# Shift product in the bank of the column sums, and the sums' logarithm and exponential ahead of the next unit's first exponential

## The chip, the cores and the metric

One core of a Trainium2 chip runs the kernel. The time is the device time of one execution in microseconds (us); three runs of the kernel before gave 409.75, 409.88 and 410.16 us, a median of 409.88 us. Engines: PE is TensorE, DVE is VectorE, ACT is ScalarE, POOL is GpSimd, SP is SyncE (here it only issues DMAs).

## What is computed

The reference is an attention with normalised queries and keys, followed by a two-layer network over its output:

```python
q_n, k_n = rmsnorm(q, g_q), rmsnorm(k, g_k)            # 8 batches, 12 heads, 448 rows, 64 wide
scores = matmul(q_n, k_n.T) / 8
attn = exp(scores - max(scores)); attn = attn / (sum(attn) + 1e-9)
x = matmul(attn, v) -> (3584, 768)
h = x @ w_in                                            # (768, 2048)
out = maximum(0.01 * h, h) @ w_out                      # (2048, 768), float32
```

## The kernel before

**Units.** The attention is cut into 24 units (`NU`): 8 batches of three groups of four heads. Unit u has seven key tiles. Scores are made transposed (keys on the partitions, queries along the row), so the sum that divides a query's row is a sum over partitions, and TensorE makes it with matmuls against ones. Every score tile covers two PSUM banks and goes through one exponential on ACT (`ex`, line 243, 128x896 elements), which writes the tile `et` to SBUF.

**The shift.** The exponentials of a unit need one number `eb`, a bound on its scores, the same on all partitions. It is made at the start of the unit from the first score tile: DVE takes the maximum of each partition (line 257), multiplies an identity matrix by it (`dg`, line 259), TensorE multiplies ones by `dg` so that all 128 maxima lie along the row on every partition (`shift_mm`, line 264), DVE takes the maximum along that row (line 274) and turns it into `eb` (line 284). The product needs 128 free columns in PSUM. For units 4 to 23 it goes into 64 spare columns (448 to 511) of each of the two banks that hold the PV product of the unit before: two matmuls of 64 columns (line 271).

**The unit before.** In the first step of unit u the kernel also ends unit u-1. `pv_slot` makes the product of `et` with the values into two banks (28 matmuls, line 400). `zcol` makes the column sums in one bank of their own, in columns 0 to 223 (line 337; up to 28 matmuls, fewer where DVE has added some tiles first in `add_e`, line 322). `pv_out` copies the PV product to SBUF (`x32`; on DVE at line 350 for the units 3 to 6, on ACT at line 352 for the others). `zcol_ln` takes the logarithm of the sums on ACT (line 358), `zcol_inv` the exponential of its negative (line 363), which is the reciprocal, and SP then issues four DMAs that spread it over the partitions into `rz` (line 368). At last x32 times rz is written to `xt` (line 378): on POOL for nine units (`xmul_pool`), on DVE for eleven (`xmul_sb`). `xt` is the input of the network.

**The network.** Its matmuls (first layer line 422, second layer line 521 and 468, late batches line 655) lie as items in a list (`queue`). After each of the four steps d = 0..3 of unit u, `fill(u, d, jobs)` runs as many items as a table (`PLAN`) says, and after each item one of `jobs`: DVE and ACT work for later units, loads and the like. Most items first call `flush()`, which issues the DVE and ACT work that earlier items put off: the additions that take products out of PSUM (line 528), and the sums `sa` of parts of the first layer's output (lines 502 to 511), which the second layer's matmuls read. In late batches an addition or a copy out of a bank (line 674) has to be done before the next product is accumulated into that bank.

**Order of the work.** The program is issued in the order in which it is written (`manual_schedule`); each engine runs its own instructions in that order, and waits on semaphores for other engines. Banks are handed out from a list of free ones: `aux()` takes one bank, `slot()` takes a pair, `drop()` gives them back at the end of the list. Instructions of different engines on the same bank wait for each other even where they touch different columns.

In the first step of unit u = 4..23 (line 1048 on) the order is: scores of tile 0, the shift's maximum and `dg`, `flush`, then the lines

```python
pv_slot(u - 1)
zcol(u - 1)
shift_mm(u)
pv_out(u - 1)
```

then `ex(u, 2)`, then `zcol_ln(u - 1)`, and then `fill` with the jobs; `zcol_inv(u - 1)` is the first job (after the first item), and `load(u + 4)`, the DMAs that fetch the queries and keys of a later unit, is the next. In the last unit (u = 23) `zcol_inv` is a job of the second step. POOL's work in this step is a small copy that waits for a transposed tile (line 290) and the DMA that loads later values (`load_v`, line 155).

Of the kernel before, what the change touches and what calls it, by code (L numbers as in the profile page):

```python
# [8 lines left out]
FP32 = mybir.dt.float32  # L9
FP16 = mybir.dt.float16  # L10
AF = mybir.ActivationFunctionType
ALU = mybir.AluOpType
AXL = mybir.AxisListType
# [5 lines left out]
def kernel(  # L19
# [11 lines left out]
    nc = tc.nc  # L31

    B, H, S, D = q.shape
    QH = 4
    NS = 7
    P = 128
    NQ = H // QH
    NU = B * NQ
# [9 lines left out]
    small = ctx.enter_context(tc.tile_pool(name="small", bufs=2))  # L48
# [39 lines left out]
    def drop(tile_):  # L88
        for i in range(8):
            if tile_ is single[i]:  # L90
                assert i not in free
                free.append(i)
                return
        x = [i for i in range(4) if tile_ is double[i]][0]
        assert 2 * x not in free and 2 * x + 1 not in free
        free.extend((2 * x, 2 * x + 1))
# [9 lines left out]
    onesp = cst.tile([P, P], FP16)  # L106
# [32 lines left out]
    st = {}  # L139
# [91 lines left out]
    def qk(u, steps):  # L231
        st[u]["sT"] = []
        for t in steps:
            sT = slot()
            score(u, t, (sT[:, 0], sT[:, 1]))
            st[u]["sT"].append((t, sT))
# [24 lines left out]
    def shift_bank(u):  # L261
        st[u]["pb"] = aux()

    def shift_mm(u):
        s = st[u]
        peak = s["spare"][:, 510:511]
        own = s.get("own")
        if own is not None or u > 0 and "pslot" in st[u - 1]:
            pb = (st[u - 1]["pslot"] if own is None else own)[:, :, S:S + 64]
            for x in range(2):  # L270
                nc.tensor.matmul(pb[:, x], onesp, s["dg"][:, 64 * x:64 * x + 64], start=True, stop=True)  # L271
            if own is not None:
                peak = small.tile([P, 1], FP32, tag="peak", name="peak")
            nc.vector.tensor_reduce(peak, pb, axis=AXL.XY, op=ALU.max)  # L274
        else:
            if "pb" not in s:
                shift_bank(u)
            pb = s["pb"]
            nc.tensor.matmul(pb[:, 0:P], onesp, s["dg"], start=True, stop=True)
            nc.vector.tensor_reduce(peak, pb[:, 0:P], axis=AXL.X, op=ALU.max)  # L280
            if u >= 3:
                drop(pb)
        s["eb"] = small.tile([P, 1], FP32, tag="eb", name="eb")
        nc.vector.tensor_scalar(s["eb"], peak, -1.0, DELTA, op0=ALU.mult, op1=ALU.add)
# [61 lines left out]
    def pv_out(u):  # L346
        s = st[u]
        s["x32"] = zpool.tile([P, 2, S], FP32, tag="x32", name="x32")
        if u in (3, 4, 5, 6):
            nc.vector.tensor_copy(s["x32"], s["pslot"][:, :, 0:S])  # L350
        else:
            nc.scalar.copy(s["x32"], s["pslot"][:, :, 0:S])  # L352
        drop(s["pslot"])

    def zcol_ln(u):
        s = st[u]
        s["zs"] = zpool.tile([P, HS], FP32, tag="zs", name="zs")
        nc.scalar.activation(s["zs"], s["zc"][:, 0:HS], AF.Ln)
        drop(s["zc"])

    def zcol_inv(u):
        s = st[u]
        nc.scalar.activation(s["zs"], s["zs"], AF.Exp, bias=0.0, scale=-1.0)
        s["rz"] = zpool.tile([P, 2, S], FP32, tag="rz", name="rz")
        for r in range(2):
            for y in range(2):
                src = s["zs"][64 * y + r:64 * y + 64:2, None, :]
                nc.sync.dma_start(s["rz"][:, r, HS * y:HS * y + HS], src.broadcast_to([32, 4, HS]))  # L368
# [421 lines left out]
    def narrow(u):  # L790
        return 3 <= u < NU - 1
# [43 lines left out]
    with tc.manual_schedule():  # L835
# [208 lines left out]
        for u in range(3, NU):  # L1044
            for d in range(4):
                if u == 5 and d == 0:
                    shared.append(u)
                if d > 0 or u > 3:
                    qk(u, (TRIPLES if tripled(u) else STEPS)[d])
                    if d == 0:  # L1050
                        shift_max(u)
                        flush()
                        if u in (5, 6):
                            xmul_sb(u - 2)
                        if narrow(u - 1):
                            pv_slot(u - 1)
                            zcol(u - 1)
                            shift_mm(u)
                            pv_out(u - 1)
                        else:  # L1060
                            zsum_slot(u - 1)
                            pv(u - 1)
                            shift_mm(u)
                            zinv(u - 1)
                    ex(u, 2)
                    if d == 0 and narrow(u - 1):
                        zcol_ln(u - 1)
                if d == 2 and (u == 3 or ADDED.get(u, 0) > 3) and u < NU - 1:
                    add_e(u)
                    if u > 4:  # L1070
                        xmul_sb(u - 1)
                jobs = []

                def job(fn, *args):
                    jobs.append(lambda: fn(*args))

                if d == 0:
                    if u == 3:
                        prep_norm(4)
                        gate(4)  # L1080
                    elif narrow(u - 1):
                        if u < NU - 1:
                            job(zcol_inv, u - 1)
                    else:
                        xmul(u - 1)
                    if u + 4 < NU:
                        job(load, u + 4)
                    if u < 5:
                        load_v(u + 3)
                    if u < 6:  # L1090
                        prep_sqp(u + 3)
                    if 5 <= u < NU - 3:
                        gate_t_of(u + 1)
                        load_v(u + 3)
                if d == 1 and narrow(u - 1) and not 5 <= u < 8 and ADDED.get(u, 0) < 4:
                    xmul_pool(u - 1)
                if u == NU - 1:
                    if d == 1:
                        job(zcol_inv, u - 1)
                if fed(u, d) and u > 3:  # L1100
                    push(u // NQ - 1)
                if (u, d) in ((3, 1), (4, 0)):
                    for ti in range(2):
                        prep_tr(u + 1, ti, VV)
                if u + 2 < NU:
                    if d == 1:
                        if ADDED.get(u) == 3 and u > 3:
                            job(lambda u: (prep_ssq(u + 2), add_e(u)), u)
                        else:
                            for ti in range(2):  # L1110
                                job(prep_ssq, u + 2, ALL, (ti,))
                if d == 1 and 5 <= u < NU - 1:
                    job(prep_g, u + 1)
                if u + 2 < NU:
                    if d == 2:
                        job(prep_rinv, u + 2)
                        if u == 6:
                            job(xmul_sb, u - 1)
                        for ti in range(2):
                            job(prep_norm, u + 2, ALL, (ti,))  # L1120
                        if u > 3:
                            job(prep_trd, u + 2)
                if d == 1 and 4 <= u < 8:
                    job(weight_sum, u - 4, 0)
                if d == 0 and 5 <= u < 9:
                    job(weight_sum, u - 5, 1)
                if d == 1 and u == NU - 2:
                    jobs.append(lambda: None)
                    job(add_e, u)
                if u == NU - 2 and d == 0:  # L1130
                    for n, tile_ in ((1, (raws, "rq", 3)), (2, (raws, "rk", 3)), (3, None), (4, (prep_p, "sq", 3))):
                        job(win_sum, n, 1, tile_)
                    for n in (3, 1, 2, 4):
                        job(x_sum, LATE, n)
                if u == NU - 1 and d == 3:
                    job(add_e, u)
                    job(xmul_sb, u - 1)
                if d == 3 and 6 <= u < NU - 3:
                    for ti in range(2):
                        job(prep_sq, u + 3, ALL, (ti,))  # L1140
                if st[u]["sT"]:
                    n = 1 if d == 1 and u % 6 == 2 else 0
                    jobs[n:n + 1] = [also(lambda: ex(u), *jobs[n:n + 1])]
                fill(u, d, jobs)
# [39 lines left out]
```

## Time and profile before

| | |
|---|---|
| median of three runs | 409.88 us |
| the profiled execution's own time | 409.67 us |
| its span, first to last instruction | 407.9 us |
| PE busy | 396.9 us (97%), clock granted 1.0 throughout |
| DVE busy | 307.1 us (75%) |
| ACT busy | 300.6 us (74%) |
| POOL busy | 72.9 us (18%) |

The profiled execution took 1.8 us more than its span. A page of the profile gives busy times of each engine, the chain of work that ended last (followed back from the last instruction), the costliest groups of instructions (a group's line, engine, operation, output and inputs; busy time and mean duration; then the idle time of the engine just before them, with what ended it), and the DMAs. The timeline lists start, duration, engine, line and operation; a bracket at the end of a line is the engine's idle time before it and what ended that. PE's records overlap: a matmul's record is longer than its distance to the next.

### The profile page before, as it was taken

What the parts mean: (1) busy time and instruction counts of PE and PEld (TensorE: products, weight loads), DVE (VectorE), ACT (ScalarE), POOL (GpSimd) and SP (SyncE); (2) the same over time, 40 slices, a digit from 0 to 9 for tenths busy, and PEclk for the clock granted to TensorE, in tenths of its full rate; (3) what the DMA queues carried; (4) which work ended last, traced back from release to release, by engine and by line L of the source; (5) the groups of instructions that cost most, each with busy time, mean ns of one, the idle gap of its engine ahead of it and who ended that gap; (6) DMA issues with size and microseconds to landing.
All of it is one profiled execution on the core that took longest, in us unless ns stands there. A gap on an engine that the chain in (4) does not pass through costs nothing.

```text
span 407.9 us, 9571 instructions
## 1 busy us (share of the span) xinstructions
PE 396.9 (97%) x3896; PEld 224.9 (55%) x3896; DVE 307.1 (75%) x481; ACT 300.6 (74%) x474; POOL 72.9 (18%) x86
## 2 busy tenths in 40 slices
PE   8999999999999999999999999999999999999996
PEld 7665454544455544555455544554455557559963
DVE  5887999959879665867679766777579888567672
ACT  5998877787978599778878689867996667743600
POOL 1887431200020200020021200021011202000000
PEclk9999999999999999999999999999999999999999
DMA  6999999898664984677664894776752560022023
GB/s 199 277 240 249 240 234 248 212 189 185 164 159 85 251 227 73 178 198 163 164 145 78 230 223 103 195 181 142 170 100 47 124 151 18 16 71 79 2 55 99
DMA packets 72526, 62.87 MB, mean 154 GB/s; under 512 B 36388, under 2 KB 67620, under 8 KB 72484
## 3 DMA queue, kind: packets, MB, share of 16 engines
q1 hardware_dynamic: 61888, 50.08, 46.8%
q0 software_dynamic: 10272, 11.80, 18.4%
q8 instruction: 30, 0.49, 0.5%
q10 hardware_dynamic: 324, 0.39, 0.3%
q14 instruction: 12, 0.10, 0.1%
HBM read 45.61 MB, written 11.01 MB: 139 GB/s over the span
## 4 chain that ended last, share of the span: by engine, by line
PE 80%; ACT 3%; DVE 3%; issue 2%; DMA 1%; SPq 1%; ACTq 0%; DVEq 0%
PE banks L422 27%; PE banks L521 23%; PE banks L228 8%; PE banks L655 6%; PE banks L400 6%; PE banks L468 6%; PE banks L337 3%; ACT et L243 1%; DMA rq<-in_q_dram 1%; SPq L368 1%; PE banks L271 1%; ACT gt L416 1%; DVE banks L257 1%; ACT sq L175 0%; PE banks L210 0%
## 5 line engine op out<-in xcount | busy, mean ns | idle before, releaser
L243 ACT ACTIVATE et<-banks,eb 128x896 f16<-128x896 f32 x168 | 161.4, 1015 | 28.9 <-PE banks L228 18.3
L422 PE MATMUL banks<-xt,win 128*128 128x448 f16 x612 | 122.4, 353 | 1.0 <-DVE xt L378 1.0
L422 PEld LDWEIGHTS <-win 128*128 128x128 f16 x612 | 57.3, 98 | 57.2 <-issue 8.0
L416 ACT ACTIVATE gt<-banks 128x448 f16<-128x448 f32 x104 | 56.4, 563 | 5.1 <-PE banks L422 3.9
L186 DVE TENSOR_REDUCE ssq<-sq 128x14 f32<-128x896 f32 (+2 forms) x49 | 50.3, 1057 | 0.7 <-ACT sq L175 0.7
L228 PE MATMUL banks<-qkT 64*64 64x448 f16 x672 | 49.3, 361 | 1.5 <-DVE qkT L810 0.8
L521 PEld LDWEIGHTS <-sa 128*128 128x128 f16 x352 | 33.4, 98 | 24.6 <-issue 3.6
L521 PE MATMUL banks<-tw,sa 128*128 128x384 f16 x264 | 46.9, 326 | 0.1
L528 DVE TENSOR_TENSOR ost<-banks,ost 128x384 f32<-128x384 f32 x55 | 30.4, 552 | 16.3 <-PE banks L521 14.3
L257 DVE TENSOR_REDUCE banks<-banks 128x1 f32<-128x896 f32 x24 | 26.3, 1097 | 14.2 <-PE banks L228 10.6
L400 PE MATMUL banks<-et,vt 64*64 64x448 f16 x672 | 36.9, 349 | 0.0
L521 PEld LDWEIGHTS <-gt 128*128 128x128 f16 x264 | 25.5, 98 | 18.7 <-issue 2.2
L468 PE MATMUL banks<-wout,gt 128*128 128x384 f16 x192 | 33.7, 327 | 0.0
L198 DVE TENSOR_TENSOR n<-rq,rinv 128x896 f16<-128x896 f32 (+2 forms) x25 | 31.0, 1241 | 3.1 <-ACT rinv L192 3.1
L228 PEld LDWEIGHTS <-qkT 64*64 64x64 f16 x672 | 16.9, 105 | 29.5 <-issue 22.5
L521 PE MATMUL banks<-wout,gt 128*128 128x384 f16 x176 | 32.4, 327 | 0.0
L290 POOL COPY gate_t<-qkT 128x1 f16<-128x1 f16 x16 | 4.8, 299 | 153.5 <-DMA qkT<-n 153.5
L378 POOL TENSOR_TENSOR xt<-x,rz 128x896 f16<-128x896 f32 x9 | 19.0, 2109 | 72.7 <-DMA rz<-zs 67.0
L352 ACT COPY x<-banks 128x896 f32<-128x896 f32 x16 | 14.5, 906 | 21.5 <-DVE banks L274 21.5
L198 DVE TENSOR_TENSOR n<-rk,rinv 128x896 f16<-128x896 f32 (+2 forms) x26 | 26.1, 1011 | 0.0
L400 PEld LDWEIGHTS <-vt 64*64 64x64 f16 x672 | 20.0, 107 | 10.0
L468 PEld LDWEIGHTS <-gt 128*128 128x128 f16 x192 | 17.8, 98 | 13.7 <-issue 2.9
(106 smaller groups left out, 484.7 us busy)
## 6 DMA issues: line engine op xcount, KB each, us to landing
rq<-in_q_dram SPq DMA_DIRECT2D x24, 448.0 KB, 4.8
rk<-in_k_dram SPq DMA_DIRECT2D x24, 448.0 KB, 5.3
out_dram<-ost SPq DMA_DIRECT2D x52, 192.0 KB, 3.4
rz<-zs SPq DMA_DIRECT2D x80, 112.0 KB, 2.8
vt<-in_v_dram POOLq DMA_DIRECT2D x24, 224.0 KB, 4.5
win<-in_moe_w_in_dram POOLq DMA_DIRECT2D x8, 384.0 KB, 14.9
wout<-in_moe_w_out_dram POOLq DMA_DIRECT2D x2, 1536.0 KB, 28.6
out_dram<-ost SPq DMA_DIRECT2D x4, 96.0 KB, 2.1
```

What stands on the lines that cost most here:

```text
L186: nc.vector.tensor_reduce(buf(u, "ssq")[:, ti, :, c[0]:c[1]], buf(u, f"sq{ti}")[:, :, c[0]:c[1]], axis=AXL.X, op=ALU.add)
L198: nc.vector.tensor_tensor(buf(u, "n16")[:, ti, c[0]:c[1]].rearrange("p s a d -> p a s d"), src[:, :, c[0]:c[1]], buf(u, "rinv")[:, ti, :, ...
L228: nc.tensor.matmul(banks[a][64 * r:64 * r + 64, 0:S].rearrange("p (t x) -> p t x", t=NS), kT(u, r, a, t), qT(u, r, a), start=True, stop=True)
L243: nc.scalar.activation(s["et"][:, t], sT[:, :, 0:S], AF.Exp, bias=s["eb"], scale=1.0)
L257: nc.vector.tensor_reduce(s["spare"][:, 511:512], sT[:, :, 0:S], axis=AXL.XY, op=ALU.max)
L400: nc.tensor.matmul(s["pv"][r][64 * a:64 * a + 64, 0:S], vts[u % NV][64 * r:64 * r + 64, a, t], s["et"][64 * r:64 * r + 64, t, a], start=(t ...
L416: nc.scalar.activation(dst, src, AF.Prelu, bias=0.0, scale=1.0, alpha=0.01)
L422: nc.tensor.matmul(hps[:, 0:S], win16[:, kt // 2, kt % 2, ts(ft, P)], xt[:, kt // 2, kt % 2], start=(kt == 0), stop=(kt == KT - 1))
L468: nc.tensor.matmul(op2[:, 0:HC], gt[:, ft, ds(col(t), P)], wout16[:, ft, ds(HC * half, HC)], start=(i == 0), stop=(i == FT - 1))
L521: nc.tensor.matmul(bank[:, 0:HC], a[:, f], b[:, f], start=(first and f == 0), stop=(f == HF - 1), skip_group_check=not first)
L528: nc.vector.tensor_tensor(dst, g[name][:, 0:HC], src, op=ALU.add)
L655: nc.tensor.matmul(bank[:, HX * i:HX * i + HX].rearrange("p (t x) -> p t x", t=NS), w, x[:, kt], start=start, stop=(kt == HK - 1), skip_gr ...
```

## The change

The shift's product of units 4 to 23 goes into the bank of the column sums of the unit before, columns 256 to 383, as one matmul of 128 columns, and DVE's maximum reads it there. The logarithm and the exponential of the column sums, with the four DMAs, are issued right after `pv_out`, ahead of `ex(u, 2)`, for all units but the last; `zcol_inv` is no longer a job of the first step, so the other jobs of that step each follow one item earlier. For u = 23 the logarithm stays behind `ex` and the exponential in the second step. The bank of the column sums is given back before that of the first score tile, so the list of free banks has another order from there on.

```diff
-        if own is not None or u > 0 and "pslot" in st[u - 1]:
-            pb = (st[u - 1]["pslot"] if own is None else own)[:, :, S:S + 64]
+        if own is not None:
+            pb = own[:, :, S:S + 64]
             for x in range(2):
                 nc.tensor.matmul(pb[:, x], onesp, s["dg"][:, 64 * x:64 * x + 64], start=True, stop=True)
-            if own is not None:
-                peak = small.tile([P, 1], FP32, tag="peak", name="peak")
+            peak = small.tile([P, 1], FP32, tag="peak", name="peak")
             nc.vector.tensor_reduce(peak, pb, axis=AXL.XY, op=ALU.max)
+        elif u > 0 and "zc" in st[u - 1]:
+            pb = st[u - 1]["zc"][:, 2 * P:3 * P]
+            nc.tensor.matmul(pb, onesp, s["dg"], start=True, stop=True)
+            nc.vector.tensor_reduce(peak, pb, axis=AXL.X, op=ALU.max)
         else:
...
                             zcol(u - 1)
                             shift_mm(u)
                             pv_out(u - 1)
+                            if u < NU - 1:
+                                zcol_ln(u - 1)
+                                zcol_inv(u - 1)
                         else:
...
                     ex(u, 2)
-                    if d == 0 and narrow(u - 1):
+                    if d == 0 and u == NU - 1:
                         zcol_ln(u - 1)
...
-                    elif narrow(u - 1):
-                        if u < NU - 1:
-                            job(zcol_inv, u - 1)
-                    else:
+                    elif not narrow(u - 1):
                         xmul(u - 1)
```

## The prediction

> **What bounds the kernel now.** I read the page first, then PE's waits, then the timelines of ACT, DVE and POOL around a unit's first step.
>
> ```profile
> span 407.9 us, 9571 instructions
> ...
> PE 396.9 (97%) x3896; PEld 224.9 (55%) x3896; DVE 307.1 (75%) x481; ACT 300.6 (74%) x474; POOL 72.9 (18%) x86
> ...
> PE 80%; ACT 3%; DVE 3%; issue 2%; DMA 1%; SPq 1%; ACTq 0%; DVEq 0%
> ...
> L352 ACT COPY x<-banks 128x896 f32<-128x896 f32 x16 | 14.5, 906 | 21.5 <-DVE banks L274 21.5
> ```
>
> PE is busy for 97% and carries 80% of the chain; ACT and DVE have a quarter of the span free. So an edit pays only where PE stands still, or costs where PE begins to. ACT's copy of the PV product waits 21.5 us in all for the shift's maximum on DVE (L274), because both use PV's banks. PE itself hardly waits; after the start (44 us) its list of waits has three entries that count:
>
> ```profile
> PE banks L422 <- DVE xt L378: 1.0, 1, 1.0
> ...
> PE banks L521 <- DVE ost L528: 0.5, 1, 0.5
> ...
> PE banks L271 <- DVE dg L259: 0.4, 1, 0.4
> ```
>
> These lie at 91, 276 and 95 us. Together they are all that a better order can win from PE.
>
> **What moves.** ACT in the first step of unit 9, before:
>
> ```profile
> 127.32 0.91 ACT L352 COPY x<-banks 128x896 f32<-128x896 f32 x1 [1.50 <-DVE banks L274]
> 128.12 1.01 ACT L243 ACTIVATE et<-banks,eb 128x896 f16<-128x896 f32 x1
> 129.03 0.36 ACT L358 ACTIVATE zs<-banks 128x224 f32<-128x224 f32 x1
> 129.41 0.39 ACT L363 ACTIVATE zs<-zs 128x224 f32<-128x224 f32 x1
> ```
>
> After the change the copy fits into the 1.50 us of idle time. The logarithm now shares a bank with the shift's maximum and waits for that (it ends at 127.23): logarithm 127.3 to 127.65, exponential to 128.05, first exponential of the scores at 127.95, where it stood at 128.12. What the copy (0.91) gave up, the pair (0.36 + 0.39 and a start between them) takes; ACT's first exponential hardly moves, and its later work moves up by some 0.75 us. The four DMAs are issued by SP behind the exponential's end, at 128.1 in place of 129.88. I worked out the exponential's end in the same way, as the maximum's end + 0.82, for the units that matter below: unit 6 81.9 (was 83.1), unit 8 112.6 (was 113.8; there ACT is busy with a square until 111.0 and the copy cannot go ahead), unit 14 205.0 (was 207.0), 18 267.4 (was 269.1), 20 298.8 (was 300.8), 22 330.9 (was 332.9). So the spread of the reciprocal is issued 1.1 to 2.0 us earlier, and with it the product x32 times rz, which waits for its landing; a quiet landing is 2.5 us after the start of the fourth issue (unit 18: issue 271.09, product 273.56). On SP nothing in front of it is late; the loads of queries and keys follow directly behind it and come 1 to 2 us earlier too, into buffers that are free; stores that stood ahead of it in two units come behind it, and nobody waits for those.
>
> **Gains.**
> (1) At 91 us PE waits for unit 5's product on DVE, and that for the spread:
>
> ```profile
> 90.60 1.09 DVE L378 TENSOR_TENSOR xt<-x,rz 128x896 f16<-128x896 f32 x1 [4.21 <-DMA rz<-zs]
> ```
>
> The issue comes 1.1 us earlier, PE stands 1.0 to 1.1 us: I take 1.1. The third of these issues took 1.99 us where 0.60 is usual, behind a transpose; if that is a full queue, nothing may be won (0). If the landing comes 2 us earlier, the wait at 95 us (0.4) goes as well. I take 1.2 of 0 to 1.5.
> (2) At 276 us PE waits for an addition that stands behind a normalisation (L198) of 2.85 us, 1.08 elsewhere. It was held by POOL's product (273.56 to 275.63). That moves up by 1.7 us and lets go at about 274: 0.6 of 0 to 0.7.
> (3) The shift's product: two matmuls of 64 columns stand 0.07 us before the next one (110.31 and 110.38); one of 128 columns takes 0.056 (48 of them in 2.85 us less one record of 0.22). 20 units by 0.012: 0.24. The Trainium skill (TensorE: Matmul & The Clock Gate, Part 1) gives N/2.4 GHz + 2.5 ns for a warm matmul, so its estimate would be 58 against 56 ns, 0.05 us in all; the row decides.
> Sum of gains 2.0.
>
> **Losses.** POOL's product and DVE's work on SBUF exclude each other. Unit 14, DVE, then POOL:
>
> ```profile
> 208.78 0.63 DVE L322 TENSOR_TENSOR ea<-et 128x896 f16<-128x896 f16 x1 [2.42 <-ACT et L243]
> 209.68 0.63 DVE L322 TENSOR_TENSOR ea<-ea,et 128x896 f16<-128x896 f16 x1 [0.27 <-ACT et L243]
> 210.22 0.45 DVE L182 TENSOR_SCALAR qkT<-qkT,gcol 128x896 f16<-128x896 f16 x1
> ...
> 212.87 0.56 DVE L528 TENSOR_TENSOR ost<-banks,ost 128x384 f32<-128x384 f32 x1
> 213.34 2.42 DVE L198 TENSOR_TENSOR n<-rq,rinv 128x896 f16<-128x896 f32 x1
> ```
>
> ```profile
> 212.69 2.12 POOL L378 TENSOR_TENSOR xt<-x,rz 128x896 f16<-128x896 f32 x1 [8.02 <-DMA rz<-zs]
> ```
>
> L198 was held until POOL's 214.81; L528, which reads a bank, ran through in 0.56. Now the product comes at about 210 (fourth issue 207.0 + 2.5 to 3.8), into a chain of SBUF work that ends in that same L528, which frees the bank for PE's product at 214.75.
> (4) Unit 14: held at 209.5, the second L322 starts at 211.6 and L528 ends 3.55 us later at 215.1; held at 210.7, at 215.4. PE waits 0.4 to 0.7: I take 0.55 of 0 to 0.75.
> (5) Unit 20 (the same chain, 302.57 on): product at 303.2 to 303.9 in place of 305.14, L528 ends at 308.9 to 309.2, was 308.55, and PE goes on at 308.60 already: 0.45 of 0 to 0.8.
> (6) Unit 8: product at 117.1 to 117.5, was 118.47, where it overlapped a copy out of a bank (L543, free of it). Now all of L182 to L528 comes behind 119.4: its end is 122.45, was 121.63, and PE goes on right behind it (121.69): 0.8 of 0 to 0.9.
> (7) Unit 22: product at about 335.4 to 336, was 338.13. DVE has no idle time from 330.24 to 337.48; all 2.07 us go into the copy L674 (ends 338.29), less 0.19 idle. PE accumulates onto that bank at 339.22: 2.07 - 0.19 - 0.93 = 0.95 of 0 to 1.0.
> (8) In units 4 to 8, 11 and 17 the first exponential comes 0.4 to 0.6 later, and three activations behind it some 0.1. PE's next scores need these banks about then (in unit 4 at 57.95, when the exponential would end at 58.0): 0.25 in all, of 0 to 0.6.
> Nine units have their product on POOL; in 9, 12, 15 and 21 the new place holds only L182 or nothing that PE waits for: 0. The eleven products on DVE keep their place in its order.
> Sum of losses 3.0. Net +1.0: 409.67 + 1.0 = 410.6 on the profiled execution; its time is 0.2 below the median of the three runs, so I forecast **410.8 us**. The bounds of the terms alone give 409.88 - 2.4 + 0 = 407.4 to 409.88 + 4.05 = 413.9.
>
> **Rivals.**
> B, faster: the spread is issued earlier and does not land earlier. POOL loads values (L155) right after the shift, in unit 14 at 203.96, and the spread, before issued at 207.0, now comes at 205.05 beside it. If it queues behind that load, the products on POOL stay within 0.9 us of their places, and (2), (4) to (7) are nil; that 0.9 decides, since at 211.65 unit 14's chain reaches a copy out of a bank and then has 1.3 us of slack. Left are 1.1 at 91 us, where the load is issued later (85.21), 0.24 and a cost of 0.1: 409.88 - 1.24 = 408.6. The Trainium skill (DMA: Bandwidth & Descriptors, Issuing engines are not separate DMA queues) says that transfers issued from different engines run on the same 16 DMA engines and interleave. If so, both run at once; as an estimate half the two transfers' time would be lost, and the product would move by about 1 us in place of 2. Against B: unit 14's landing, the slowest of POOL's, took 3.8 us (issue 208.89, product 212.69) where the quiet one took 2.5, so even 1.3 us more would leave 0.7 to 2 us of the move.
> C, no change: the spread lands so early that POOL's product falls into the idle time before the chain. DVE idles from 206.36 to 208.78 in unit 14 and from 300.15 to 302.57 in unit 20. A start before 207.5 and 301.2 costs nothing there, and (4) and (5) go: 409.88 + 1.0 - 1.0 = 409.9. Against it: the fourth issue alone starts at 207.0. Any other two of the losses missing end here as well.
> D, much slower: the change makes ACT late and not early. Where ACT has no idle time before the maximum, the pair stands in front of the scores' exponential, and PE's scores wait for banks. The terms at (8) then stand at 0.1 to 0.2 in most of 19 units: 1.5 more, 412.3. Against it: in 13 of 16 copies ACT idled before.
> That the change doesn't do what it says can be left out: in the order of the built program the pair stands ahead of the exponential on ACT, and the product in the sums' bank.
>
> **How the numbers follow.** A 0.42, B 0.20, C 0.28, D 0.10. Under 0.2% (0.8 us) a change cannot be told from none here. A and D are slower by more than that, though A only just; C is within; B is faster. The range takes in half of D and nearly all of B: 408.4 to 412.3.
>
> **What would show it.** Right: L378 on POOL 1 to 2 us earlier against the reductions of its unit; L322, L182 or L502 of 2 to 2.6 us; new entries in PE's waits for L528 in units 8, 14 and 20 and for L674 in unit 22; no wait at 91 us and none at 276. Wrong: POOL's products in their old places (B), or entries of PE L228 for ACT L243 in many units (D).

## The result, and the profile after

Six runs of the changed kernel gave 412.36 to 412.79 us, a median of **412.43 us**; six of the kernel before, beside them, 408.81 to 410.18, a median of 409.81. The ratio is 1.0064, 95% interval 1.0049 to 1.0079: slower. The forecast was +0.9 us with a range of 408.4 to 412.3; measured were +2.6. In a later series the ratio of the same two kernels was 1.0046 (1.0030 to 1.0062).

The profiled execution of the changed kernel took 412.50 us. Its lines carry numbers higher by 3 from L275 to L1059: L378 is now L381, L502 and L505 are L505 and L508, L521 is L524, L528 is L531, L674 is L677. From its page, the span and the shares of the chain; from its groups of lines on ACT, the copy and the logarithm (busy time, mean; idle time before, with what ended it):

```profile
span 410.7 us, 9529 instructions
...
PE 82%; DVE 5%; ACT 2%; issue 1%; DVEq 0%; ACTq 0%
```

```profile
L355 ACT COPY x<-banks 128x896 f32<-128x896 f32 x16 | 14.7, 918 | 4.4 <-PE banks L403 4.3
...
L361 ACT ACTIVATE zs<-banks 128x224 f32<-128x224 f32 x20 | 7.3, 365 | 11.6 <-DVE banks L277 11.6
```

The copy's 21.5 us of waiting for the shift's maximum are gone (what is left, 4.4, is for PE's product); 11.6 us of such waiting now stand in front of the logarithm. The chain has 5% on DVE, where it had 3%. PE's list of waits has new entries (us in all, times, longest):

```profile
PE banks L524 <- DVE sa L508: 3.7, 3, 1.5
...
PE banks L658 <- DVE u L677: 0.5, 1, 0.5
```

The entries at 91, 95 and 276 us are gone, as predicted; L658 in unit 22 is there, as predicted. The first line was not predicted: PE waits three times for the second of the sums `sa`, not for the addition L531 (before: L528).

**Where the time came from.** I put PE's matmuls of the two profiles side by side and took the change of start (after less before) wherever it jumps. Start of the kernel, before unit 3: +0.41, in matmuls that the change does not touch (this differs from execution to execution). 91 us: -1.08. 95 us: -0.43. Unit 8 (118.82 before): +1.72. Unit 14 (212.02): +1.22. Unit 18 (277.11): -0.78. Unit 20 (305.81): +1.22. Unit 22 (339.22): +0.65, and 0.29 behind it in unit 23. Small steps are left, none over 0.2 and together -0.4. The sum is +2.83, which is the difference of the two profiled executions. So the three waits for `sa` cost 4.16 us, more than all gains together.

Unit 14 in the timeline, DVE, then POOL, then PE:

```profile
209.90 0.62 DVE L325 TENSOR_TENSOR ea<-ea,et 128x896 f16<-128x896 f16 x1 [0.27 <-ACT et L243]
210.44 2.27 DVE L182 TENSOR_SCALAR qkT<-qkT,gcol 128x896 f16<-128x896 f16 x1
212.63 0.41 DVE L505 TENSOR_TENSOR sa<-gt 128x512 f16<-128x512 f16 x1
213.07 0.42 DVE L508 TENSOR_TENSOR sa<-sa,gt 128x512 f16<-128x512 f16 x1
```

```profile
210.17 2.29 POOL L381 TENSOR_TENSOR xt<-x,rz 128x896 f16<-128x896 f32 x1 [5.04 <-DMA rz<-zs]
```

```profile
211.69 0.81 PE L524 MATMUL banks<-tw,sa 128*128 128x384 f16 x4
213.55 0.82 PE L524 MATMUL banks<-tw,sa 128*128 128x384 f16 x4 [1.05 <-DVE sa L508]
```

Four matmuls of the item `i1` read the first half of `sa`, which was made in an earlier step. The fifth reads the second half, which DVE makes at that very time. POOL's product came at 210.17; DVE's L182 (0.45 us elsewhere) was held until 212.71; the two sums came behind it, and PE stood from its fourth to its fifth matmul. In the kernel before, the same place looks like this on PE:

```profile
211.37 1.46 PE L521 MATMUL banks<-tw,sa 128*128 128x384 f16 x8
```

Eight matmuls without a gap. DVE's two sums stood here (in the kernel before, L505 is the second one):

```profile
210.84 0.43 DVE L502 TENSOR_TENSOR sa<-gt 128x512 f16<-128x512 f16 x1 [0.17 <-ACT gt L416]
211.30 0.42 DVE L505 TENSOR_TENSOR sa<-sa,gt 128x512 f16<-128x512 f16 x1
```

PE's fifth matmul began at 212.02, and the sum L505 that it reads had ended at 211.73. A matmul that waits for this sum begins 0.05 us behind it (213.50 and 213.55 above). So the slack was 0.29 - 0.05 = 0.24 us, and it is the same in units 8 (118.53, 118.82) and 20 (305.52, 305.81). With it the losses can be worked out: measured against PE's own work, the sum ended 1.93, 1.45 and 1.47 us later than before; less 0.24 that makes 1.69, 1.21 and 1.23, against 1.72, 1.22 and 1.22 measured.

### The profile page after: what moved, and what is told of

It is laid out like the page before. It is cut to its first block, busy times and chain, and to the rows that moved or that the text cites. A ratio compares the mean times of both kernels' runs of the same rounds, so it can differ in the third digit from the quotient of the medians.

```text
span 410.7 us, 9529 instructions
## 1 busy us (share of the span) xinstructions
PE 397.3 (97%) x3876; PEld 224.6 (55%) x3876; DVE 312.2 (76%) x481; ACT 304.0 (74%) x474; POOL 73.3 (18%) x86
## 4 chain that ended last, share of the span: by engine, by line
PE 82%; DVE 5%; ACT 2%; issue 1%; DVEq 0%; ACTq 0%
PE banks L425 26%; PE banks L524 23%; PE banks L228 8%; PE banks L471 8%; PE banks L403 7%; PE banks L658 6%; PE banks L340 3%; DVE qkT L182 1%; ACT et L243 1%; PE banks L276 1%; DVE sa L505 1%; DVE ws L627 1%; DVE xs L644 0%; PE banks L210 0%; ACT gt L419 0%
## 5 line engine op out<-in xcount | busy, mean ns | idle before, releaser
L419 ACT ACTIVATE gt<-banks 128x448 f16<-128x448 f32 x104 | 55.2, 551 | 8.9 <-PE banks L425 7.4
L186 DVE TENSOR_REDUCE ssq<-sq 128x14 f32<-128x896 f32 (+2 forms) x49 | 50.3, 1058 | 1.0 <-ACT sq L175 1.0
L524 PE MATMUL banks<-tw,sa 128*128 128x384 f16 x264 | 47.4, 326 | 3.7 <-DVE sa L508 3.7
L524 PEld LDWEIGHTS <-sa 128*128 128x128 f16 x352 | 33.2, 98 | 29.3 <-DVE sa L508 4.8
L531 DVE TENSOR_TENSOR ost<-banks,ost 128x384 f32<-128x384 f32 x55 | 30.5, 554 | 14.7 <-PE banks L524 13.4
L524 PEld LDWEIGHTS <-gt 128*128 128x128 f16 x264 | 25.5, 98 | 18.0 <-issue 1.4
L524 PE MATMUL banks<-wout,gt 128*128 128x384 f16 x176 | 32.4, 326 | 0.0
L381 POOL TENSOR_TENSOR xt<-x,rz 128x896 f16<-128x896 f32 x9 | 19.2, 2130 | 67.3 <-DMA rz<-zs 47.2
L198 DVE TENSOR_TENSOR n<-rq,rinv 128x896 f16<-128x896 f32 (+2 forms) x25 | 26.4, 1057 | 2.8 <-ACT rinv L192 2.8
L198 DVE TENSOR_TENSOR n<-rk,rinv 128x896 f16<-128x896 f32 (+2 forms) x26 | 26.2, 1012 | 0.0
L559 ACT COPY ost<-banks 128x384 f32<-128x384 f32 x11 | 5.3, 480 | 26.8 <-PE banks L524 26.8
```

The lines of the kernel that those rows point to most:

```text
L186: nc.vector.tensor_reduce(buf(u, "ssq")[:, ti, :, c[0]:c[1]], buf(u, f"sq{ti}")[:, :, c[0]:c[1]], axis=AXL.X, op=ALU.add)
L198: nc.vector.tensor_tensor(buf(u, "n16")[:, ti, c[0]:c[1]].rearrange("p s a d -> p a s d"), src[:, :, c[0]:c[1]], buf(u, "rinv")[:, ti, :, ...
L419: nc.scalar.activation(dst, src, AF.Prelu, bias=0.0, scale=1.0, alpha=0.01)
L524: nc.tensor.matmul(bank[:, 0:HC], a[:, f], b[:, f], start=(first and f == 0), stop=(f == HF - 1), skip_group_check=not first)
L531: nc.vector.tensor_tensor(dst, g[name][:, 0:HC], src, op=ALU.add)
```

## Experiments

Theory (POOL): the loss is POOL's earlier product, which holds up DVE's work on SBUF just ahead of the sums. Rivals: ACT's new order makes the sums' inputs late (ACT); the product's new bank and the new order of free banks cost the time (bank). Times of the kernel before in the three series: 410.16, 409.84 and 409.90 us. "In before's time" below means: less the drift of PE up to there. The edits are shown against the changed kernel, shortened, with `...` where lines are left out.

One reading serves all of them. In every profile a product on POOL that is not held on purpose begins 0.16 to 0.31 us behind the landing of the last transfer of the spread that it needs, and 0.17 in units 8, 14 and 20. So the landing sets its place, also where the bracket of its line names an ACT instruction, whose semaphore happened to change last.

### The shift's product alone

```diff
-                            if u < NU - 1:
-                                zcol_ln(u - 1)
-                                zcol_inv(u - 1)
...
-                    if d == 0 and u == NU - 1:
+                    if d == 0 and narrow(u - 1):
                         zcol_ln(u - 1)
...
+                    elif narrow(u - 1):
+                        if u < NU - 1:
+                            job(zcol_inv, u - 1)
```

> The shift's product in the column sums' bank for all units, logarithm and exponential in their old places (behind the first exponentials; first job). Theory (POOL): the 2.6 us come from POOL's product x32*rz, which moved in front of DVE's sums sa in units 8, 14 and 20 and so makes PE late at the second layer's second item. Here ACT's copy no longer waits for the maximum, so the first exponential and the logarithm behind it come some 0.7 us earlier, and the product by at most that: 117.8 in unit 8 (was 118.47, the sum L505 began at 118.11) and 304.4 in unit 20 (the sum L502 began at 304.63), which costs 1.3 to 1.5 us each, but 212.0 in unit 14, behind that chain (ended 211.73), which costs nothing. Gains 0.24 for the product, 0.7 to 1.1 at 91 and 95 us, 0.5 at 276 us. Together 409.8 - 1.6 + 2.8 = 411.0, or 409.6 if the products stay where they were. Rival (bank): the single bank and its order in the list of free banks cost the time: 412.4 already here, with waits in other places. Rival (ACT): the pair ahead of the exponentials makes ACT's outputs late: nothing of the loss here, 409.6 or less.

Measured: 414.19 us (411.97 to 415.91), ratio 1.0089 (1.0060 to 1.0118). This is 4.0 above before, where the theory had 1.2. It is more than the whole change costs (1.0064) by the medians, though the two intervals overlap. 1.6 us of its profile come from the start of the kernel again. The rest is in the same places: +1.70 in unit 8, +1.59 in 14, +1.60 in 20, +0.70 and +0.30 in 22 and 23, -0.79 in unit 18. Unit 14, DVE and POOL:

```profile
212.96 0.45 DVE L182 TENSOR_SCALAR qkT<-qkT,gcol 128x896 f16<-128x896 f16 x1
213.69 2.34 DVE L505 TENSOR_TENSOR sa<-gt 128x512 f16<-128x512 f16 x1 [0.28 <-ACT gt L419]
216.07 0.42 DVE L508 TENSOR_TENSOR sa<-sa,gt 128x512 f16<-128x512 f16 x1
```

```profile
213.68 2.07 POOL L381 TENSOR_TENSOR xt<-x,rz 128x896 f16<-128x896 f32 x1 [5.05 <-ACT gt L419]
```

I expected the product behind the sums (212.0 in before's time); it came at 210.74. The exponential of the sums ended 0.7 us earlier, as expected; the other 1.3 are the landing: the slowest of unit 14's four spreads took 3.6 us from issue to landing in the profile of before (median 2.4) and 3.0 here, and from the fourth issue to the product it was 3.8 us and is 2.5. I had taken a slow landing for unit 14's normal place. The gains at 91 and 95 us are missing because the copy of units 3 to 6 is DVE's, so nothing moves on ACT there. So the logarithm and exponential need not move at all: freeing ACT's copy from the maximum is enough to bring the product in front of the sums. ACT's order is the old one here, so the rival (ACT) has no cause left; the rival (bank) is not yet out.

### The logarithm and exponential alone

```diff
-        elif u > 0 and "zc" in st[u - 1]:
-            pb = st[u - 1]["zc"][:, 2 * P:3 * P]
-            nc.tensor.matmul(pb, onesp, s["dg"], start=True, stop=True)
-            nc.vector.tensor_reduce(peak, pb, axis=AXL.X, op=ALU.max)
+        # as before: two matmuls of 64 columns into st[u - 1]["pslot"]
```

(The last line stands for the code before.)

> Logarithm and exponential ahead of the first exponential, the shift's product in the PV banks' spare columns as before. Theory (POOL): the copy again waits for the maximum, so the pair ends some 0.9 us later than in the changed kernel and 0.9 earlier than before; the product comes at about 117.6 in unit 8 and 304.2 in unit 20 (held sums, 1.4 us each) and 211.7 in unit 14 (little); gains at 91 and 276 us of 1.2; the first exponential comes 0.8 late in every unit, which costs 0 to 1.5 at the score banks: 410.5 to 412. Rival (bank): the old time or better, 409.8, since banks and product are as before. Rival (ACT): more than the changed kernel, 413 or more, with long waits of PE for banks read by ACT's exponentials.

Measured: 414.29 us (413.70 to 414.56), ratio 1.0106 (1.0085 to 1.0127): 4.1 above before, where the theory had 0.7 to 2.2. From the list of PE's waits (the lines are before's):

```profile
PE banks L521 <- DVE sa L505: 3.7, 3, 1.4
PE banks L228 <- ACT et L243: 1.9, 6, 0.6
```

The same three waits for the sums stand here with the old banks and the old product: the rival (bank) is out for them. The second line is the cost that the prediction priced in its step (8) and its rival D: the pair stands between the copy, which waits for the maximum again, and the first exponential, so PE's scores wait for banks: by PE's starts 0.7 us more than before in each of units 12 and 18 (175.44 and 268.53 us). In the changed kernel that line reads 0.7, 4, 0.2, as it did before the change. I had expected little in unit 14; it was +1.42, since the product came at 210.2 in before's time.

### Three units as before, and the three alone

```diff
-                            if u < NU - 1:
+                            if u < NU - 1 and u not in (8, 14, 20):
                                 zcol_ln(u - 1)
                                 zcol_inv(u - 1)
```

(with the logarithm, the job and the product's banks of these three units as before; the second kernel turns the condition round: `if u in (8, 14, 20)`.)

> The changed kernel with the units 8, 14 and 20 as before in all parts (product in the PV banks' spare columns, logarithm behind the first exponentials, exponential as first job). Theory (POOL): the three waits of PE for the second half of the sums (1.7, 1.2 and 1.2 us) go, everything else stays: 412.43 - 4.16 = 408.3, faster than both. Rival (bank): the loss is spread over the units, three of twenty give back 0.4: 412.0. Rival (ACT): 408.3 too if ACT's order in these three units makes the sums late; the next kernel tells it from the first.

> The kernel before with the whole change in units 8, 14 and 20 alone. Theory (POOL): the three waits for the sums (1.7, 1.2, 1.2 us) and no gain, since the waits at 91, 95 and 276 us belong to units 6 and 18: before + 4.1 us. Rival (bank or ACT order, spread over all units): three of twenty units, before + 0.4.

Measured: 408.67 us, ratio 0.9972 (0.9959 to 0.9985), for the first, and 413.15 us, ratio 1.0080 (1.0057 to 1.0103), for the second: 1.5 us below before where 1.5 were expected, and 3.3 above where 4.1 were. In the first PE has no entry for `sa` any more. In the second (its lines are one higher than the changed kernel's)

```profile
PE banks L525 <- DVE sa L509: 3.8, 3, 1.4
...
PE banks L426 <- DVE xt L382: 0.8, 1, 0.8
```

the three waits are there and the gain at 91 us is not. The change in three of twenty units makes the whole loss. Both fit (POOL) and (ACT).

### POOL's product held behind the second sum

```diff
+                    if u in (8, 14, 20):
+                        held.append(u - 1)
+                    else:
+                        xmul_pool(u - 1)
...
                 fill(u, d, jobs)
+                if d == 1 and held:
+                    nc.gpsimd.tensor_copy(gate_t, sa[:, 1, HF - 1, P - 1:P])
+                    xmul_pool(held.pop())
```

> The changed kernel; in units 8, 14 and 20 POOL first copies one element of the second half of the sums sa (written by the second sum, L508) and only then multiplies, so the product cannot come before these sums. ACT's order, banks and DMAs as in the changed kernel. Theory (POOL): 412.43 - 4.16 = 408.3, no wait of PE for sa in these units, the sums 0.42 long. Rival (ACT) and rival (bank): 412.4, since only POOL's work moves.

Measured: 409.66 us, ratio 0.9992 (0.9979 to 1.0005). The edit moves nothing but POOL's product, and most of the loss came back: 3.1 us by the ratios, 2.5 between the two profiles. The entry for `sa` is gone; what is left of the loss is in another line:

```profile
PE banks L524 <- DVE ost L531: 1.6, 4, 0.5
```

```profile
210.57 0.55 DVE L546 COPY ost<-banks 128x384 f32<-128x384 f32 x1
211.03 2.33 DVE L511 TENSOR_TENSOR sa<-gt 128x512 f16<-128x512 f16 x1
213.29 0.41 DVE L514 TENSOR_TENSOR sa<-gt,sa 128x512 f16<-128x512 f16 x1
213.63 0.54 DVE L531 TENSOR_TENSOR ost<-banks,ost 128x384 f32<-128x384 f32 x1
```

The product (211.01 to 213.08) now holds the third sum (in unit 8 the fourth), and the addition L531 behind it is late for PE by 0.39, 0.52 and 0.48 us (units 8, 14, 20). The fourth entry is in unit 15, whose product is not held: one of its spreads took 5.3 us to land (4.1 at most in the changed kernel's profile), and PE lost 0.33. This is the wait that the prediction had put into the changed kernel, at 0.8, 0.55 and 0.45; it appears once the earlier wait is taken away. (ACT) and (bank) are out: they had 412.4.

### The product cut in two

```diff
-                    xmul_pool(u - 1)
+                    if u in (8, 14, 20):
+                        held.append(u - 1)
+                        xmul_pool(u - 1, r=slice(0, 1))
...
+                if d == 2 and held:
+                    nc.gpsimd.tensor_copy(gate_t, sa[:, 3, HF - 1, P - 1:P])
+                    xmul_pool(held.pop(), r=slice(1, 2))
```

> The changed kernel; in units 8, 14 and 20 POOL's product is cut into two of 448 columns: the first at once, the second behind the last of the sums (a copy of one element of it on POOL holds it back). Theory (POOL holds DVE's two-input work for the whole of its own instruction): the held sum takes about 0.42 + 1.05 in place of 2.3 to 2.5 us, the three waits shrink by 1.05 each: changed kernel - 3.1 us, that is before - 0.5. If DVE were slowed in some other way (sharing, or the product's DMAs), the waits would stay or go as a whole: changed kernel - 0 or - 4.2.

Measured: 408.82 us, ratio 0.9979 (0.9968 to 0.9990), 0.5 us below the expectation. Unit 8, where DVE began a sum just as POOL began its half product; POOL first:

```profile
116.95 1.12 POOL L381 TENSOR_TENSOR xt<-x,rz 128x448 f16<-128x448 f32 x1 [6.26 <-DMA rz<-zs]
```

```profile
116.96 1.40 DVE L508 TENSOR_TENSOR sa<-sa,gt 128x512 f16<-128x512 f16 x1
118.28 0.54 DVE L546 COPY ost<-banks 128x384 f32<-128x384 f32 x1
```

In the changed kernel a whole product held a sum in unit 8. DVE, then POOL:

```profile
116.56 2.35 DVE L505 TENSOR_TENSOR sa<-gt 128x512 f16<-128x512 f16 x1 [0.17 <-ACT gt L419]
```

```profile
116.57 2.07 POOL L381 TENSOR_TENSOR xt<-x,rz 128x896 f16<-128x896 f32 x1 [6.05 <-ACT gt L419]
```

Alone such a sum takes 0.42. It was held for 0.98 us by the half product (1.12) and for 1.93 by the whole one (2.07): the hold shrank by as much as POOL's instruction. In all profiles a held sum ends 0.28 us behind POOL's record, a held L325 (0.62 alone) 0.48 and a held L198 (1.08 alone) 0.95: each time its own length less about 0.14. So DVE's operation stands until POOL is as good as through and then takes its own time; had the two shared at half speed, a sum would have taken, by estimate, 0.84 us (2 x 0.42) beside either product. PE lost 0.75 in unit 8 (1.72 before the cut) and nothing in 14 and 20, where holds of 0.7 and 0.6 (L325, 1.31 and 1.20) used up slack that was there. The halving is not the only difference: the first half needs only two of the four spreads, so it began about 0.5 us earlier than the whole one in units 14 and 20 (209.3 and 302.8 in before's time, against 209.8 and 303.3), and in unit 8 it met the second sum, not the first. What the halving alone is worth to PE is not shown.

The Trainium skill (SBUF — State Buffer, Who interferes with whom) says that a VectorE instruction with two SBUF inputs contends with a GpSimd one that reads SBUF, and, of VectorE's 2-port modes: "Whoever issues first gets the shared pair for the whole instruction; the other fully blocks". These rows agree for two inputs (L505, 2.35). L182 has one, and was held too (2.27); the page counts its operation among those that can run in a 2-port mode, which no run here shows.

### The gains alone

```diff
-                            if u < NU - 1:
+                            if u in (6, 18):
                                 zcol_ln(u - 1)
                                 zcol_inv(u - 1)
```

(with the other units as before in all parts.)

> The kernel before with the whole change in units 6 and 18 alone. Theory (POOL): the gains alone, 1.5 us at 91 and 95 us and 0.7 to 0.8 at 276 us: before - 2.2 us. Rival (the spread does not land earlier, the gains are chance): before.

Measured: 407.95 us (407.55 to 408.34), ratio 0.9952 (0.9938 to 0.9966): 1.9 below before where 2.2 were expected. PE's starts jump by -1.13, -0.43 and -0.78 at 91, 95 and 276 us and nowhere else by more than 0.1 behind the start. The gains of steps (1) and (2) are these two units.

### Held behind the fourth sum, and in unit 22

```diff
+                if d == (1 if u == 22 else 2) and held:
+                    nc.gpsimd.tensor_copy(gate_t, st[u]["ea"][:, 1, S - 1:S] if u == 22 else sa[:, 3, HF - 1, P - 1:P])
+                    xmul_pool(held.pop())
```

> The changed kernel; POOL's product held behind the fourth sum (second half, L514) in units 8, 14 and 20, and behind the second addition of the exponentials (L325) in unit 22, where copies out of banks follow on DVE. Theory (POOL): no wait for the sums, no wait for the addition L531 either (the kernel held behind the second sum paid 0.4 to 0.5 us three times there), and none at unit 22's copy (0.65 + 0.3): changed kernel - 5.1 us, before - 2.5. Rival for unit 22 (its wait comes from DVE's full row of work and not from the product): before - 1.5.

Measured: 408.96 us, ratio 0.9974 (0.9959 to 0.9989): 0.9 to 1.1 below before where 2.5 were expected. All waits that were meant to go are gone, unit 22's and the one in unit 23 too (-0.69 and -0.29 against the changed kernel), so these belong to POOL's product. A new one stands in units 9, 15 and 21:

```profile
PE banks L276 <- DVE dg L259: 1.2, 3, 0.4
```

```profile
118.79 2.91 DVE L198 TENSOR_TENSOR n<-rq,rinv 128x896 f16<-128x896 f32 x1
```

The normalisation L198 is held by 1.8 us, DVE's row of work behind it has too little idle time to catch up, and the next unit's shift is late by 0.4. The hold moves down the row until idle time takes it up.

### Two halves behind two sums, or three units as before with unit 22 held

The first cuts the product in units 8, 14 and 20 and holds its halves behind the second and the fourth sum, unit 22 as above:

```diff
+                if d in (1, 2) and held:
+                    nc.gpsimd.tensor_copy(gate_t, sa[:, 2 * d - 1, HF - 1, P - 1:P])
+                    xmul_pool(held[0] if d == 1 else held.pop(), r=slice(d - 1, d))
```

The second is the kernel with these three units as before, with unit 22's hold.

> The changed kernel; in units 8, 14 and 20 POOL's product is cut in two halves of 448 columns, the first held behind the second sum (L508), the second behind the fourth (L514), so that each begins beside an instruction of DVE that reads a bank; in unit 22 the whole product is held behind the second addition of the exponentials. Theory (POOL): no wait for sums, additions or copies in these four units, and the normalisation behind is held by half as long as in the kernel held behind the fourth sum, so its waits of 0.4 us for dg in units 9, 15 and 21 go too: changed kernel - 4.16 - 0.94, before - 2.5 us. Rival (each hold only moves the wait to the next consumer): before - 1.2, as the whole product held behind the fourth sum.

> Units 8, 14 and 20 as before, all others changed, and in unit 22 POOL's product held behind the second addition of the exponentials. Theory (POOL): the kernel with these three units as before (before - 1.5 us) less unit 22's wait and what followed it (0.75 + 0.27): before - 2.5 us. Rival: the same as without the hold, before - 1.5.

Measured: 408.14 us (408.09 to 408.65), ratio 0.9956 (0.9942 to 0.9971), and 408.39 us, ratio 0.9958 (0.9944 to 0.9972). Both are 1.5 to 1.8 below before, where 2.5 were expected. In the first the waits for `dg` are not gone but smaller (0.8 us in all). In the second, unit 22's wait is gone and the 0.26 behind it in unit 23 stays; 0.38 appeared at the addition in unit 8. These two and the kernel with units 6 and 18 alone are faster than both kernels, and their intervals do not tell them apart.

### The changed kernel once more

> The changed kernel once more on this chip: before + 2.6 us, with the three waits for the sums of 1.5, 1.0 and 1.1 us in the same places.

Measured: 412.03 us (410.61 to 412.92), ratio 1.0046 (1.0030 to 1.0062): 2.1 above before where 2.6 were expected. The profiled execution took 410.98 us and shows only two of the three waits:

```profile
PE banks L524 <- DVE sa L508: 2.2, 2, 1.1
...
PE banks L524 <- DVE ost L531: 0.3, 1, 0.3
```

In unit 8 the sums came through, and the product held the third one. DVE, then POOL:

```profile
116.32 0.43 DVE L505 TENSOR_TENSOR sa<-gt 128x512 f16<-128x512 f16 x1 [0.17 <-ACT gt L419]
116.78 0.42 DVE L508 TENSOR_TENSOR sa<-sa,gt 128x512 f16<-128x512 f16 x1
117.12 0.55 DVE L546 COPY ost<-banks 128x384 f32<-128x384 f32 x1
117.59 2.16 DVE L511 TENSOR_TENSOR sa<-gt 128x512 f16<-128x512 f16 x1
```

```profile
117.39 2.07 POOL L381 TENSOR_TENSOR xt<-x,rz 128x896 f16<-128x896 f32 x1 [5.35 <-ACT uu L191]
```

The slowest of unit 8's four spreads took 4.9 us from issue to landing here and 4.1 in the first profile. So one kernel meets PE's sum in one execution and not in the next, which is worth 1.4 us between the two profiles (1.73 less 0.36 for the wait at L531).

## Why the prediction was wrong

**The mechanism was right, and the places too.** In before's time the products on POOL came at 117.7, 209.8, 303.3 and 335.4 us in units 8, 14, 20 and 22; predicted were 117.1 to 117.5, about 210, 303.2 to 303.9 and 335.4 to 336. Three lie where the text put them, unit 8's 0.2 us behind. The held instructions (L182 in units 14 and 22, L325, before L322, in unit 20, L505, before L502, in unit 8) are of the lines the text names.

**The step that failed** is the consumer in (4), (5) and (6): "a chain of SBUF work that ends in that same L528, which frees the bank for PE's product at 214.75". I followed DVE's chain to its last instruction and asked when PE needs that. PE reads an earlier link, the sum L505, at 212.02 in unit 14, with 0.24 us to spare. The three terms were 0.55, 0.45 and 0.8, together 1.8; they measured 1.22, 1.22 and 1.72, together 4.16. The bounds of these terms (0.75, 0.8 and 0.9) were too low for the same reason.

**The other terms.** (1) 1.2 predicted, 1.5 measured, with both waits gone. (2) 0.6, measured 0.78. (3) 0.24, measured 0.03: from the start of the shift's product to the start of the next matmul it is 0.068 us before and 0.066 to 0.067 after, so the 0.056 of a row of equal matmuls did not carry over to a single one, and the text's other estimate, 0.05, was nearer. (7) 0.95 in unit 22, measured 0.65, and 0.29 more in unit 23 that no step had. (8) 0.25, measured nothing: the copy really goes ahead of the maximum, and the score banks' waits stay at 0.7 us. With the right sum for (4) to (6) the same working gives 1.0 - 1.8 + 4.16 = +3.4, or +2.8 with the measured sizes of all terms, and +2.4 with the small steps of -0.4 that no term had; +2.4 is what PE's starts show behind the start of the kernel (2.83 - 0.41).

**The rivals.** B fails: the products of units 8, 14, 18, 20 and 22 moved by 0.8 to 2.8 us. Its price fails too: it let a move of up to 0.9 us cost nothing, and unit 8's 0.8 cost 1.72. Its argument has something to it, though. The spread's median from issue to landing grew (last column of the list of DMA issues; before, then after):

```profile
rz<-zs SPq DMA_DIRECT2D x80, 112.0 KB, 2.8
```

```profile
rz<-zs SPq DMA_DIRECT2D x80, 112.0 KB, 3.5
```

The load of the values beside it went from 4.5 to 5.4 us. The Trainium skill (DMA: Bandwidth & Descriptors, Issuing engines are not separate DMA queues) says that transfers of different engines interleave; both numbers agree with that. C needed a product before 207.5 in unit 14 and did not get it. D's number, 412.3, is close to the result by chance, since it came from another mechanism; its own is seen only with the logarithm and exponential alone.

**What stays open.** The spread of before's own times (408.2 to 413.0 us in one series) was not taken apart. In its profile the product of unit 8 begins 0.06 us before the sum L505 ends and the one of unit 20 0.05 us behind that sum's start, so I take it that a landing a little earlier brings the collision there too; that is argued from the two places and from the two profiles of the changed kernel, not shown. The kernel with the two held halves varied little, 408.09 to 408.65, but two that hold the whole product did not (409.17 to 410.68 and 408.51 to 409.92), so that holding it removes the spread is not shown.

## What to carry to other kernels

When a chain on one engine is pushed back, check every link of it for its own reader, not only the last: the reader with the least slack sets the cost, and a consumer that shows no wait may be 0.2 us from one. An off-path product that arrives earlier is a gain only if the place it arrives in is idle on the engine that it excludes; it is cheapest to let only those units arrive early for which somebody waits. And one profile gives one landing of a transfer: a place 1.3 us behind the usual is not a margin to build on.

## What the runs showed of the hardware

- While POOL multiplies from SBUF, DVE's element by element operations on SBUF stand for the rest of POOL's instruction, with one input (L182, 2.27 in place of 0.45 us) as with two (L505, 2.35 in place of 0.42). The held one ends its own length, less 0.14 us (0.20 for L182), behind POOL's record. Copies and additions out of banks run beside it in their usual 0.55 us.
- A reduction that reads SBUF does not exclude POOL's product: in unit 21 of the changed kernel DVE's L186 ran from 320.82 for its usual 1.07 us, and the product that began beside it at 321.22 took its usual 2.08. Where a sum of two SBUF inputs was first by 0.05 us (unit 20 of the kernel before), the product took 2.32.
- POOL got its turn between two DVE instructions that follow each other directly. In unit 14 of the changed kernel its product's record begins at 210.17, while DVE's addition L325 runs until 210.52, and lasts 2.29 where 2.07 is usual; the next instruction of DVE, L182, was held, and POOL was not held behind it.
- The start of the kernel differed by up to 1.6 us between profiled executions, in matmuls that no edit touches; drifts are best read from a point behind it.
